# Unread products of the identity on TensorE, ahead of the first round and behind two packs of each of the first eight blocks

## The chip, the cores and the metric

The kernel runs on one core of one Trainium2 chip. The metric is device time in microseconds (us) of one execution, with all loads from and stores to device memory in it. The core has five engines with a queue each: PE (TensorE, matmuls; its weight loads are shown apart as PEld), DVE (VectorE), ACT (ScalarE), POOL (GpSimd) and SP (SyncE, which here only issues transfers). An engine takes the instructions of its queue in order and waits for others by semaphores. PE reads from SBUF and writes to PSUM only.

## The reference

Two parts follow each other. The first is a gated linear recurrence with a 40 x 40 state for each of 4 x 8 (batch, head) pairs over 768 steps; the second is a feed-forward block whose gate mixes along the sequence.

```python
for t in range(S):                                   # S = 768, D = 40
    m_new = np.maximum(f_gate[:, :, t] + m, i_gate[:, :, t])
    f_stab, i_stab = np.exp(f_gate[:, :, t] + m - m_new), np.exp(i_gate[:, :, t] - m_new)
    C = f_stab * C + i_stab * einsum('bhd,bhe->bhde', vt, kt)
    n = f_stab * n + i_stab * kt
    y[:, :, t] = sigmoid(o_gate[:, :, t]) * (C @ qt) / max(abs(n @ qt), 1)
x = y as (4, 768, 320)
h = relu(x @ w_in); u, v = halves of h               # 320 -> 2 x 512
v_n = (v - mean(v)) / sqrt(var(v) + 1e-6)
v_s = einsum('ts,bsd->btd', w_spatial, v_n) + b_spatial
out = (u * v_s) @ w_out                              # 512 -> 320
```

All tensors are float32.

## The kernel before

The recurrence is worked in blocks of 128 steps: 4 batches of 6 blocks, numbered n = 0 to 23, each of two sub-blocks of 64 steps and 8 heads. A block n passes through these packs of small matmuls on PE, and through DVE, ACT and POOL between them:

- `pe_ex(n)` (L364): one matmul of 128 x 512 whose result is the exponent of the weights of the block; ACT makes W from it (L401), POOL scales the keys by W (`ktw`, L406).
- `pe_s(n)` (L370): 16 products of keys and queries into SX; DVE multiplies them by W into KS (`keys`, L415).
- `pe_dc(n)` (L379): 16 products of scaled keys and values into DX, which are the changes of the states; DVE adds them to the decayed states ST (`step`, L431 and L433), which POOL has decayed (L423).
- `pe_intra(n)` (L387): 16 products of KS and values into DX.
- `pe_inter(n)` (L396): 16 products of queries and states into SX.
- `rows(n)` on DVE (L441 reads SX, L445 reads DX), `norm(n)` (L451 to L459), `gated(n)` on POOL (L465, L467), then `turn(n)` (L478): three transposes on PE into px, read by ACT (L484, xH) and DVE (L490, xL).

SX and DX are two PSUM tiles of two banks each, with 512 columns a bank; they have one copy. In SX the products of `pe_s` take columns 0 to 255 of both banks and those of `pe_inter` columns 256 to 419; columns 420 to 511 are used by nothing.

The second part has `a_v` (L528, matmuls of 128 x 512 into pv), a normalisation over DVE, ACT and POOL (L535 to L559), `b_pu` (L570) and `b_pb` (L579 to L581, 128 x 384), and `c_out` (L603 to L605). Its weights are loaded as 64-bit numbers and split into a high and a low half on ACT, DVE and POOL (`conv`, L261 to L283) and `split` (L296 to L298) while the first blocks run. The first `a_v` comes at 67.7 us, the first `b_pb` at 94.4 us.

Ahead of block 0 stand the gates: scans on DVE, then `gates_decay1(z)` for the two halves z of the sequence, which puts three transposes (L175) and one product (L177) on PE, and transfers through device memory that lay the gates out for `pe_ex`.

The order is written out by hand: every function is a generator that yields between instructions, all of them stand in a list `stages`, and a table of numbers, ORDER, says whose next step is issued. Each engine's queue holds its instructions in that order. Waits are found from the tiles: an instruction waits for the earlier ones of other engines that wrote what it reads or read what it writes.

Of the kernel before, what the change touches and what calls it, by code (L numbers as in the profile page):

```python
# [37 lines left out]
def mlstm_moe(ctx: ExitStack, tc: tile.TileContext, a):  # L38
    nc = tc.nc
# [6 lines left out]
    def bank(shape, name):  # L46
        return ps.tile(shape, F32, name=name, tag="pm", bufs=4)


    ident = const.tile([128, 128], F32, name="ident")  # L50
# [114 lines left out]
    def gates_decay1(z):  # L165

        ez = eg[:, z * hs:z * hs + hs]
        dg = wk.tile([128, NB, 16], F32, name="dg", tag="dg", bufs=1)[0:BH]
        nc.gpsimd.tensor_tensor(
            out=dg, in0=ez.rearrange("p (c t) -> p c t", t=L)[:, :, L - 1:L].broadcast_to([BH, NB, 16]),  # L170
            in1=pick[:, 0:16].unsqueeze(1).broadcast_to([BH, NB, 16]), op=ALU.mult)
        yield
        pe = bank([128, 512], "pe")
        for i in range(NB // 2):
            nc.tensor.transpose(pe[:, i * BH:(i + 1) * BH], ez[:, i * 128:(i + 1) * 128], ident[0:BH, 0:BH])  # L175
        pd = pe[:, 128:128 + NB * 16]
        nc.tensor.matmul(pd, pick[:, 16:144], dg.rearrange("p c x -> p (c x)"), start=True, stop=True)  # L177
        dec_[z] = pe, pd

    dec_ = {}  # L180
# [138 lines left out]
    SX = ps.tile([128, 2, 512], F32, name="SX", tag="SX", bufs=1)  # L319
# [4 lines left out]
    intra_ = DX[:, :, 256:256 + HH * E]  # L324
    PAIRS = ((0, 0), (1, 0), (0, 1), (1, 1))

    def rh_v(t):
        return t[:, 0:VW].rearrange("p (h d) -> p h d", h=H)

    def rh_k(t):  # L330
        return t[:, VW:VW + KW].rearrange("p (h d) -> p h d", h=H)
# [4 lines left out]
    def half(p):  # L336
        return slice(64 * p, 64 * p + 64)

    def feat(p):
        return slice(64 * p, 64 * p + D)  # L340
# [32 lines left out]
    def pe_dc(n):  # L373
        rh = RH[n % NRH]
        for j in range(HH):
            for hf, e in PAIRS:
                if n % NB < NB - 1 or e == 0:
                    h, r = hf * HH + j, half(e ^ hf)
                    nc.tensor.matmul(  # L379
                        dc_[feat(hf), e, j * E:(j + 1) * E], rh_k(rh)[r, h], rh_v(rh)[r, h], start=True, stop=True)  # L380

    def pe_intra(n):
        rh, ks = RH[n % NRH], KS[n % NKS]
        for j in range(HH):
            for hf, e in PAIRS:
                h, r = hf * HH + j, half(e ^ hf)
                nc.tensor.matmul(intra_[half(e), hf, j * E:(j + 1) * E], ks[r, h], rh_v(rh)[r, h], start=True, stop=True)  # L387

    def state(n, e):
        return ZS if n % NB == 0 and e == 0 else ST[(2 * n + e) % NST]  # L390
# [101 lines left out]
    def pe_pack(n):  # L492

        if n + 2 < N:
            pe_ex(n + 2)
        if n + 1 < N:
            pe_dc(n + 1)
        if n >= 0:
            pe_intra(n)
        if n + 2 < N:  # L500
            pe_s(n + 2)
        if n >= 0:
            pe_inter(n)
# [132 lines left out]
    def pack(n):  # L636
# [5 lines left out]
        if n + 1 < N:  # L642
            do(pe_dc, n + 1)
            do(step, n + 1, 0)
            do(decay, n + 1, 1)
        if n >= 0:
            do(pe_intra, n)
# [42 lines left out]
    for z in range(2):  # L690
        do(gates_max, z, V)
        do(gates_sum, z)
        do(gates_parts, z, V)
        do(store_g, z, SP)
        do(gates_low, z, V)
        do(load_a_near, z, 0, AQ)
        do(load_a_near, z, 1, PQ)
        if z == 0:
            do(load_g, 0, SP)
            do(load_g, 1, SP)  # L700
            do(load_rh, 1)
            do(load_qk, 2)
        do(gates_exp, z)
        do(gates_decay1, z)
        do(gates_decay2, z)
# [12 lines left out]
    do(weights, 1)  # L718
    do(load_g, 3, SP)
    do(pe_dc, 0)  # L720
    do(pe_s, 1)
    do(step, 0, 0)
# [71 lines left out]
    n, prev = 7, (0, 0, 0)  # L794
# [131 lines left out]
```

## Time and profile before

| | us |
|---|---|
| runs | 377.08, 378.86, 427.2 |
| median of the runs | 378.86 |
| profiled execution, its own time | 378.9 |
| its span, first to last instruction | 377.1 |
| PE busy in the span | 330.6 (88%) |
| PE weight loads busy | 298.9 |
| DVE busy | 220.1 |
| ACT busy | 144.8 |
| POOL busy | 111.7 |
| mean granted TensorE clock, as recorded | 0.982 |

The span is the time in which instructions ran; 1.8 us of the execution's own time lie around it. Busy times are sums over the span, and since the kernel has stages with different limits, they are to be read stage by stage. A matmul's busy time holds its way through the array, so matmuls overlap, and the distance between the starts of neighbours tells what one costs in a row. The granted clock is made from records of its changes; a stretch ahead of the first record shows 1.00 whatever the clock was, so durations of like instructions have to be read beside it.

### The profile page before, as it was taken

What the parts mean: (1) busy time and instruction counts of PE and PEld (TensorE: products, weight loads), DVE (VectorE), ACT (ScalarE), POOL (GpSimd) and SP (SyncE); (2) the same over time, 40 slices, a digit from 0 to 9 for tenths busy, and PEclk for the clock granted to TensorE, in tenths of its full rate; (3) what the DMA queues carried; (4) which work ended last, traced back from release to release, by engine and by line L of the source; (5) the groups of instructions that cost most, each with busy time, mean ns of one, the idle gap of its engine ahead of it and who ended that gap; (6) DMA issues with size and microseconds to landing.
All of it is one profiled execution on the core that took longest, in us unless ns stands there. A gap on an engine that the chain in (4) does not pass through costs nothing.

```text
span 377.1 us, 10595 instructions
## 1 busy us (share of the span) xinstructions
PE 330.6 (88%) x4426; PEld 298.9 (79%) x4426; DVE 220.1 (58%) x552; ACT 144.8 (38%) x335; POOL 111.7 (30%) x178
## 2 busy tenths in 40 slices
PE   0215685989699999999999999999999999999996
PEld 0104574756678899989899999889899998999996
DVE  6556869569779877345767454447675234614231
ACT  6256214267624332367332322663321216701211
POOL 5156645256535244111423232123331101200000
PEclk9999999989869999999999999999999999999999
DMA  7856244554251324300233414002100100100101
GB/s 200 253 155 224 82 127 138 161 171 128 67 170 55 127 86 145 105 2 18 78 94 123 142 56 141 1 20 73 56 2 2 54 1 0 54 0 0 51 5 52
DMA packets 16047, 32.24 MB, mean 85 GB/s; under 512 B 4028, under 2 KB 8920, under 8 KB 16000
## 3 DMA queue, kind: packets, MB, share of 16 engines
q1 hardware_dynamic: 15456, 31.30, 27.3%
q8 instruction: 35, 0.57, 0.6%
q0 software_dynamic: 416, 0.15, 0.2%
q10 hardware_dynamic: 128, 0.12, 0.1%
q14 instruction: 12, 0.10, 0.1%
HBM read 27.19 MB, written 4.33 MB: 84 GB/s over the span
## 4 chain that ended last, share of the span: by engine, by line
PE 80%; DVE 7%; DMA 5%; POOL 3%; issue 2%; SPq 1%; ACT 1%; POOLq 0%; DVEq 0%; ACTq 0%
PE pv L528 12%; PE pu L570 12%; PE pb L579 10%; PE pb L581 9%; PE pb L580 9%; PE DX L387 4%; PE SX L396 4%; PE pc L603 4%; PE pc L605 4%; PE pc L604 4%; PE SX L370 3%; PE px L478 3%; DMA w<-in_w_in 2%; PE DX L379 2%; DMA QK<-in_qk 2%
## 5 line engine op out<-in xcount | busy, mean ns | idle before, releaser
L579 PE MATMUL pb<-wsH,vH 128*128 128x384 f32 x192 | 69.0, 359 | 0.7 <-DVE g L587 0.7
L580 PE MATMUL pb<-wsL,vH 128*128 128x384 f32 x192 | 65.2, 339 | 0.0
L581 PE MATMUL pb<-wsH,vL 128*128 128x384 f32 x192 | 65.0, 339 | 0.0
L591 ACT CAST big<-g 128x384 fp32r<-128x384 f32 x32 | 16.4, 513 | 95.3 <-DVE g L589 93.2
L587 DVE TENSOR_TENSOR g<-pb,bsp 128x384 f32<-128x384 f32 x32 | 17.8, 556 | 43.0 <-PE pb L581 42.7
L579 PEld LDWEIGHTS pb<-wsH,vH 128*128 128x128 f32 x192 | 36.3, 189 | 2.6 <-DVE g L587 1.0
L580 PEld LDWEIGHTS pb<-wsL,vH 128*128 128x128 f32 x192 | 36.5, 190 | 0.2
L581 PEld LDWEIGHTS pb<-wsH,vL 128*128 128x128 f32 x192 | 36.4, 190 | 0.0
L545 POOL TENSOR_TENSOR st<-st,half_neg 128x1 f32<-128x1 f32 x24 | 14.7, 619 | 67.5 <-DVE st L543 64.5
L570 PE MATMUL pu<-xH,wiH 128*128 128x384 f32 x96 | 33.1, 345 | 0.4 <-DVE xL L490 0.4
L423 POOL TENSOR_TENSOR ST<-ST,DEC 104x164 f32<-104x164 f32 x40 | 21.9, 548 | 37.5 <-DVE ST L433 24.7
L528 PE MATMUL pv<-wiH,xH 128*128 128x512 f32 x72 | 30.0, 428 | 0.0
L603 PE MATMUL pc<-woH,big 128*128 128x320 f32 x96 | 29.8, 311 | 0.0
L605 PE MATMUL pc<-woH,big 128*128 128x320 f32 x96 | 29.6, 308 | 0.0
L604 PE MATMUL pc<-woL,big 128*128 128x320 f32 x96 | 29.6, 308 | 0.0
L387 PEld LDWEIGHTS DX<-RH,KS 64*64 64x64 f32 x768 | 15.6, 154 | 13.8 <-DVE ST L433 7.6
L387 PE MATMUL DX<-RH,KS 64*64 64x41 f32 x768 | 18.6, 248 | 8.8 <-DVE ST L433 6.9
L401 ACT ACTIVATE W<-ex 128x512 f32<-128x512 f32 x24 | 14.3, 595 | 31.2 <-PE ex L364 19.0
L406 POOL TENSOR_TENSOR RH<-RH,W 128x320 f32<-128x320 f32 x24 | 17.7, 738 | 28.4 <-ACT W L401 27.7
L370 PE MATMUL SX<-QK 40*64 40x64 f32 x768 | 20.9, 258 | 5.1 <-DVE KS L415 4.7
L484 ACT ACTIVATE xH<-px 128x384 fp32r<-128x384 f32 x24 | 11.8, 490 | 34.4 <-PE px L478 34.3
L415 DVE TENSOR_TENSOR KS<-SX,W 128x512 f32<-128x512 f32 x24 | 16.5, 686 | 14.5 <-PE DX L387 9.5
(120 smaller groups left out, 766.3 us busy)
## 6 DMA issues: line engine op xcount, KB each, us to landing
RH<-in_vk SPq DMA_DIRECT2D x24, 484.0 KB
QK<-in_qk SPq DMA_DIRECT2D x48, 160.0 KB
out<-ot SPq DMA_DIRECT2D x24, 160.0 KB
big<-in_w_sp SPq DMA_DIRECT2D x6, 384.0 KB
w64b<-in_w_out SPq DMA_DIRECT2D x4, 320.0 KB
w<-in_w_in SPq DMA_DIRECT2D x4, 256.0 KB
w64b<-in_w_in SPq DMA_DIRECT2D x4, 256.0 KB
w<-in_w_rem SPq DMA_DIRECT2D x2, 256.0 KB
```

What stands on the lines that cost most here:

```text
L370: nc.tensor.matmul(s_[half(e ^ hf), hf, j * L:(j + 1) * L], QK[feat(hf), e, 0, j], QK[feat(hf), e, 1, j], start=True, stop=True)
L387: nc.tensor.matmul(intra_[half(e), hf, j * E:(j + 1) * E], ks[r, h], rh_v(rh)[r, h], start=True, stop=True)
L423: nc.gpsimd.tensor_tensor(out=ST[(2 * n + e + 1) % NST][0:HI], in0=state(n, e)[0:HI], in1=DEC[0:HI, 2 * k + e, b * HH:(b + 1) * HH].unsque ...
L528: nc.tensor.matmul(pm, l, r, start=i == 0, stop=i == len(terms) - 1)
L570: nc.tensor.matmul(pu, w, x, start=i == 0, stop=i == len(terms) - 1)
L579: nc.tensor.matmul(pb, vH[:, cd], wsH[hf][:, s], start=s == 0, stop=False)
L580: nc.tensor.matmul(pb, vH[:, cd], wsL[hf][:, s], start=False, stop=False)
L581: nc.tensor.matmul(pb, vL[:, cd], wsH[hf][:, s], start=False, stop=s == NB - 1)
L587: nc.vector.tensor_tensor(out=g, in0=pb_[(b, hf, d)], in1=bsp[:, hf * 384:hf * 384 + 384], op=ALU.add)
L603: nc.tensor.matmul(pc, gH[:, c], woH[:, d], start=d == 0, stop=False)
L604: nc.tensor.matmul(pc, gH[:, c], woL[:, d], start=False, stop=False)
L605: nc.tensor.matmul(pc, gL[:, c], woH[:, d], start=False, stop=d == 3)
```

## The change

A function `busy(m)` puts m matmuls of the identity with 92 of its own columns into the unused columns of SX's first bank. Nothing reads the result. It is called with 26 at the end of `gates_decay1(1)`, and with 4 at the end of `pe_dc(n)` and of `pe_intra(n)` for n below 8: 26 + 16 x 4 = 90 products, which are 180 matmuls on PE, since each product of float32 operands is two matmuls with a weight load each (L177 shows it). No `yield` is added, so ORDER fits as it is, and PE's queue is otherwise the same.

```diff
@@ gates_decay1
         nc.tensor.matmul(pd, pick[:, 16:144], dg.rearrange("p c x -> p (c x)"), start=True, stop=True)
+        if z == 1:
+            busy(26)
         dec_[z] = pe, pd
@@ ahead of rh_v
+    def busy(m):
+
+        for _ in range(m):
+            nc.tensor.matmul(SX[:, 0, 420:512], ident, ident[:, 0:92], start=True, stop=True)
+
@@ pe_dc, at its end
+        if n < 8:
+            busy(4)
@@ pe_intra, at its end
+        if n < 8:
+            busy(4)
```

Lines of the changed kernel are numbered 2 to 11 higher than those of the kernel before (L370 is L377, L379 is L386, L387 is L396, L396 is L407, L364 is L371, L415 is L426, L441 is L452); `busy` is L332.

PE's queue at the start. In the kernel before, the last product of the gates is followed by the exponents of blocks 0 and 1 (ex), the keys by queries of block 1, the states' changes of block 0 (DX from RH) and the keys by queries of block 2:

```order
L177 MATMUL pe<-dg,pick 128x96
L364 MATMUL ex<-GM_76,AT_73 128x512
L364 MATMUL ex<-GM_77,AT_73 128x512
L370 MATMUL SX<-QK_107 64x64 x16
L379 MATMUL DX<-RH_102 40x41 x16
L370 MATMUL SX<-QK_108 64x64 x16
```

In the changed kernel:

```order
L177 MATMUL pe<-dg,pick 128x96
L332 MATMUL SX<-ident 128x92 x26
L371 MATMUL ex<-GM_76,AT_73 128x512
L371 MATMUL ex<-GM_77,AT_73 128x512
L377 MATMUL SX<-QK_107 64x64 x16
L386 MATMUL DX<-RH_102 40x41 x16
L332 MATMUL SX<-ident 128x92 x4
L377 MATMUL SX<-QK_108 64x64 x16
```

The 26 products wait for nothing new and stand ahead of both exponents; four more stand between the states' changes of block 0 and the next pack.

PE's queue around block 1, with the waits of each instruction. Before, the states' changes of block 2 (RH_104) are followed by intra of block 1 and by inter of block 2, whose first matmul waits for DVE:

```order
L379 MATMUL DX<-RH_104 40x41 [waits DVE_49,Pool_49]
L379 MATMUL DX<-RH_104 40x41 x15
L387 MATMUL DX<-RH_103,KS_101 64x41 [waits DVE_49]
L387 MATMUL DX<-RH_103,KS_101 64x41 x15
L396 MATMUL SX<-ST_115,QK_108 64x41 [waits DVE_49]
```

In the changed kernel:

```order
L386 MATMUL DX<-RH_104 40x41 [waits DVE_49,Pool_49]
L386 MATMUL DX<-RH_104 40x41 x15
L332 MATMUL SX<-ident 128x92 x4
L396 MATMUL DX<-RH_103,KS_101 64x41 [waits DVE_49]
L396 MATMUL DX<-RH_103,KS_101 64x41 x15
L332 MATMUL SX<-ident 128x92 [waits DVE_49]
L332 MATMUL SX<-ident 128x92 x3
L407 MATMUL SX<-ST_115,QK_108 64x41 [waits DVE_49]
```

Here the products behind intra wait for DVE themselves, since their columns lie between the first and the last column that DVE's last reading of SX spans; the same holds behind intra of blocks 3 and 7.

DVE's queue at the keys of block 1 (KS_101). Before, the multiplication waits for ACT's W alone:

```order
L431 COPY ST_112<-DX 104x164 [waits PE_49]
L280 TENSOR_TENSOR bits<-bits,wiH 64x256 [waits Activation_49]
L415 TENSOR_TENSOR KS_101<-SX,W 128x512 [waits Activation_49]
L433 TENSOR_TENSOR ST_113<-DX,ST_113 104x164 [waits Pool_49]
L298 TENSOR_TENSOR wsL_95<-big,wsH_93 128x384 [waits DMAHW0_49,DVE_49,Activation_49]
```

In the changed kernel:

```order
L442 COPY ST_112<-DX 104x164 [waits PE_49]
L282 TENSOR_TENSOR bits<-bits,wiH 64x256 [waits Activation_49]
L426 TENSOR_TENSOR KS_101<-SX,W 128x512 [waits PE_49,Activation_49]
L444 TENSOR_TENSOR ST_113<-DX,ST_113 104x164 [waits Pool_49]
L300 TENSOR_TENSOR wsL_95<-big,wsH_93 128x384 [waits DMAHW0_49,DVE_49,Activation_49]
```

It now waits for the four products behind the states' changes of block 0 as well. Two later multiplications into KS and two readings of SX by L441 have got such a wait on PE too; their order on DVE is unchanged.

## The prediction

> **What bounds the kernel now.** I read the page's busy shares by slice first, then PE's busy time in stretches of time, then single matmuls, to see at which clock they ran. The page shows PE and the recorded clock in 40 slices of 9.4 us each:
>
> ```profile
> PE   0215685989699999999999999999999999999996
> ...
> PEclk9999999989869999999999999999999999999999
> ```
>
> From about 113 us on PE is full to the end. What the first 113 us lose or gain is therefore added to the end nearly one for one. The stages, each engine's busy time with the number of instructions, then the clock and the transfers:
>
> ```profile
> 20.70:28.27 7.57, 0.00 (x1) 0.03 (x1) 4.72 (x13) 3.81 (x12) 4.30 (x7) 1.00 0.65 179
> 28.27:44.64 16.37, 10.09 (x293) 8.13 (x293) 13.06 (x31) 8.06 (x19) 10.58 (x14) 1.00 0.49 158
> 44.64:62.24 17.60, 12.29 (x301) 10.11 (x301) 13.30 (x33) 5.75 (x13) 8.50 (x15) 1.00 0.48 139
> 62.24:76.48 14.24, 13.35 (x164) 10.09 (x164) 8.23 (x22) 3.63 (x9) 4.08 (x6) 1.00 0.50 152
> ...
> 83.31:100.38 17.07, 13.62 (x195) 10.29 (x195) 16.17 (x41) 11.62 (x28) 10.70 (x16) 1.00 0.32 84
> ```
>
> Before 28 us PE waits for the gates. From 28 to 62 us PE (22.4 of 34.0 us) and DVE (26.4) take turns, from 62 to 76 us PE is the bound, and from 83 to 100 us DVE is (16.2 of 17.1). Now the clock. Three matmuls of one shape, start and duration:
>
> ```profile
> 73.42 0.63 PE L528 MATMUL pv<-wiH,xH 128*128 128x512 f32 x1
> ...
> 81.56 0.63 PE L528 MATMUL pv<-wiH,xL 128*128 128x512 f32 x1
> ...
> 83.83 0.39 PE L528 MATMUL pv<-wiH,xH 128*128 128x512 f32 x1
> ```
>
> The second ran at a recorded 0.50 and the third at 1.00 (rows below). The first is as slow as the second, though the column says 1.00: nothing is recorded ahead of the first change. So PE ran at half speed until about 76 us, and the change's 90 unread products can be meant for nothing but this clock, or cost time. The records change on a grid of 3.41 us, so I cut PE's busy time along it:
>
> ```profile
> 69.66:73.07 3.41, 3.41 (x39) 1.00 0.18 59
> 73.07:76.48 3.41, 3.41 (x9) 1.00 0.72 203
> 76.48:79.90 3.42, 1.59 (x97) 1.00 0.49 148
> 79.90:83.31 3.41, 3.41 (x52) 0.50 0.72 243
> ...
> 100.38:103.79 3.41, 3.41 (x97) 0.50 0.31 126
> 103.79:107.21 3.42, 3.42 (x69) 0.50 0.28 78
> 107.21:110.62 3.41, 3.41 (x42) 0.50 0.84 241
> ```
>
> Two things are to be seen. A full window need not raise the clock: those from 69.66, 100.38 and 103.79 were full, held many small matmuls, and left it low; those from 73.07, 79.90 and 107.21, with mostly wide ones, were followed by a high clock. And a window with 1.59 of 3.42 us busy was followed by a low one, though its longest gap was the 1.8 us of the waits below.
>
> **What a product costs.** The nearest rows are the gates' product, float32 with the same 128 weight columns and 96 instead of 92 columns moving, and the transposes:
>
> ```profile
> 19.96 0.52 PE L177 MATMUL pe<-dg,pick 32*128 32x96 f32 x1
> ...
> 19.96 0.74 PE L177 MATMUL pe<-dg,pick 32*128 32x96 f32 x2
> ...
> 54.87 0.90 PE L478 MATMUL px<-ident,x 128*128 128x128 f32 x3
> 55.42 0.78 PE L364 MATMUL ex<-GM,AT 84*128 84x512 f32 x1
> ```
>
> L177's first matmul ends at 20.48 and the second at 20.70: 0.22 us each at the low clock, rounded to 0.43 a product. Bounds: two transposes' distance, 2 x (55.42 - 54.87)/3 = 0.37 us, and the pair alone from start to end, 0.74, which counts the way through the array that followers share. I take 0.43, since shape and type are L177's; at the high clock half, 0.21, as pv's duration falls. Four are 1.7 us low, 0.9 high.
>
> **The 26 at the start.** They need only the identity, which L175 has used, and begin behind L177's second matmul at about 20.3 us. At the low clock they take 26 x 0.43 = 11.2 us, to 31.5. Their cover is PE's wait for a transfer, up to 28.27, and behind it the next cover is ACT:
>
> ```profile
> 28.27 1.19 PE L364 MATMUL ex<-GM,AT 84*128 84x512 f32 x2 [7.57 <-DMA GM<-scr_g]
> ...
> 30.13 0.59 ACT L401 ACTIVATE W<-ex 128x512 f32<-128x512 f32 x1
> ```
>
> ex would start 3.2 us late. ACT takes it at 30.13, and could have done so from about 28.9 (0.6 us for the first of the two), so 1.2 us of the 3.2 are hidden and W is 2.0 late; with it the keys on DVE and everything behind them. If the clock rises after some 5 us of the 26, they end near 28.5 and cost nothing. I take 2.0.
>
> **The 16 packs.** Behind the states' changes or intra the four products run in PE's next wait, if there is one. The waits of PE from 28.27 to 62.24 us, then from 62.2 to 101 us (total, times, longest):
>
> ```profile
> PE SX L370 <- DVE KS L415: 4.7, 3, 2.0
> PE DX L387 <- DVE ST L433: 2.9, 3, 1.4
> PE SX L396 <- DVE xs L441: 1.5, 1, 1.5
> PE DX L379 <- POOL RH L406: 1.2, 1, 1.2
> PE SX L396 <- DVE KS L415: 0.9, 1, 0.9
> PE px L478 <- POOL x L467: 0.4, 1, 0.4
> ...
> PE DX L387 <- DVE ST L433: 4.0, 2, 3.1
> PE DX L387 <- DVE ST L431: 1.8, 1, 1.8
> ```
>
> Blocks 0 to 3: 8 packs of 1.7 us are 13.7. Cover: 4.7 less the 2.0 ahead of the first pack and less about 1.0 that stands behind ex (the keys that end it are made from that ex, so the wait moves along); 2.9; 1.5; 0.4. That is 6.5. The 0.9 is none, because there the products wait for the same DVE instruction first. On the path: 13.7 - 6.5 = 7.2 us. New waits come with it: the keys and L441 on DVE wait for products they don't read, and behind them stand the states' changes on DVE and then POOL.
>
> Blocks 4 to 7: the packs behind changes 5, 6 and 7 and intra 4, 5, 6 and 7 (the eighth, behind changes 4, fell into the part above). Five at the low clock, two (changes 6, intra 6) at the high: 5 x 1.7 + 2 x 0.9 = 10.3. Cover: 1.2 and 0.9 (the first of the 4.0), and 0.9 where DVE is the bound behind intra 6. The 1.8 is no cover, since the pack of changes 6 stands ahead of block 7's keys by queries, for which DVE waits first. On the path 7.3 us.
>
> Back comes some clock: a window like that from 76.48 is filled by 0.9 us more and may keep the clock (half of 3.4 us), and the gap of 3.1 us ahead of 100 may fall across two windows (half of 10.2). I count 2.5 of these 6.8.
>
> Sum: 2.0 + 7.2 + 7.3 - 2.5 = 14.0 us on the profiled execution's own 378.9 (span 377.1 and 1.8 around it), which lies 0.04 above the median of the runs: 393 us. No transfer is added, none moves in SP's or POOL's queue; loads that wait for a buffer go later with the blocks, and none is late for PE in these rows.
>
> This rests on the clock not staying high, and here I weigh a rule. Between 28.3 and 34 us PE would hold, at the high clock, ex 0.6, two packs of 16 at 0.5 and four products, about 2.5 us in 5.7: less than the 47% of the window after which the clock fell. So even if the 26 raise it, I expect it to fall there. The Trainium skill, "TensorE: Matmul & The Clock Gate", Part 1: The HAM clock gate, says that the low clock is the default, that some 3.4 us of sustained matmuls release it, and that an idle window brings it back. By that rule the 26 would raise it and gaps of 2 us would not end it, which gives the first rival's time. The rows agree on the default and the window's length; on the release, three full windows disagree, and on the fall the window from 76.48 does, which was not idle.
>
> **The rivals.** First, faster: the clock rises during the 26 and stays. Its place is the gap from 28.3 to 34 us, and it decides whether the clock survives that. For it: the 26 leave PE no gap, as in the windows that raised it; against it: the three full windows, and the fall. Price: the start costs nothing; PE's and DVE's turns from 28 to 62 us gain about 3.3 (PE's share of a round halves by some 2.3 us a block, the products give 1.7 back, DVE keeps the rest); 62.24 to 76.48 gains half of 13.35, 6.7; 79.90 to 83.31 gains 1.7; seven packs at 0.9 cost 6.0; half of a chance at the 5.1 from 100.38 on is 2.5. Together -8.2: 371 us.
>
> Second, no change: the products cost less than L177 says, because the weights are the same each time, and fall into waits. For it: the waits of 28 to 62 us sum to 11.5. With 0.2 a product, at either clock, 16 packs are 13 us, 10 of them hidden; with 1 or 2 us of clock won, 378 to 383 us.
>
> Third, the change does nothing to PE's order but lengthen it, with the clock raised for a few us at the start: the forecast without its 2.0, 391. I count it with the forecast.
>
> **How the numbers follow.** Forecast with the third: 0.57; its own range is 384 (all the clock comes back, 0.37 a product) to 402 (none comes back and DVE's new waits take half the cover). Faster rival: 0.30, from 366 to 377. Second: 0.13. A measurement of this kernel tells 2% from no change, so the marks are 371.3 and 386.5. Faster by over 2%: 0.20 from the first rival and 0.02 from the second. Slower: 0.54 of the 0.57. The rest, 0.24, within. The range of 370 to 401 leaves out a third of the first rival (0.11) and 0.05 at the top.
>
> **What would show it.** Right: pv at 0.63 us in its first eight, DX and SX packs of 16 around 1.1 us from 30 to 60 us; ex of block 0 starting near 31.5; `busy` lines near 0.4 us apart; the first b_pb later than 94.4 us by about 14. Wrong: packs of 0.7 us and pv of 0.39 from the first one on, ex at 28.3, and PE's waits for DVE longer than before; then the clock stayed high and the first rival holds. If packs are slow and the end comes within 4 us, the waits hid more than 6.5.

## The result and the profile after

| us | before | after |
|---|---|---|
| median of 4 runs each | 377.97 | 400.1 |
| lowest to highest of the undisturbed runs | 376.03 to 378.86 | 396.41 to 400.26 |
| ratio, with its 95% interval | | 1.057 (1.046 to 1.068) |
| span of the profiled execution | 377.1 | 394.6 |
| PE busy in it | 330.6 | 360.5 |

The changed kernel is slower by 5.7%. The second row and the ratio leave out one run of each kernel, 427.2 before and 402.62 after, which lie over 1.5% above the fastest of their kernel. The profiled execution is the fastest of its four: its span grew by 17.5 us, while the medians lie 22 apart. The page's lines that answer to those quoted ahead, busy PE and the recorded clock in 40 slices, here of 9.9 us each:

```profile
PE 360.5 (91%) x4606; PEld 329.6 (84%) x4606; DVE 218.8 (55%) x552; ACT 145.2 (37%) x335; POOL 111.3 (28%) x178
...
PE   0298798998969999999999999999999999999996
...
PEclk9999999998986999999999999999999999999999
```

PE is nearly full from the third slice on, where before it had waits between 28 and 62 us. It is full of unread products and not of more useful work, as PE's timeline shows (start, duration; in brackets the idle time ahead and who ended it):

```profile
20.48 11.40 PE L332 MATMUL SX<-ident 128*128 128x92 f32 x52
31.59 1.20 PE L371 MATMUL ex<-GM,AT 84*128 84x512 f32 x2
33.78 1.13 PE L377 MATMUL SX<-QK 40*64 40x64 f32 x32 [0.99 <-DVE KS L426]
34.68 0.77 PE L386 MATMUL DX<-RH 64*40 64x41 f32 x32
35.38 2.01 PE L332 MATMUL SX<-ident 128*128 128x92 f32 x8
38.25 1.14 PE L377 MATMUL SX<-QK 40*64 40x64 f32 x32 [0.85 <-DVE KS L426]
```

The 26 products take 11 us, ex follows at 31.6, and a pack of 16 small products (x32, two matmuls each) still takes 1.1 us: the clock is low, as it was. The same place in the chain of work that ended last (start, duration):

```profile
35.45 1.96 PE SX L332 x8
37.41 0.03 issue
37.46 0.04 issue
37.51 0.70 DVE KS L426
...
40.75 1.96 PE SX L332 x8
42.70 0.02 issue
42.73 0.50 DVE xs L452
```

A pack of four unread products stands on the chain (in what follows, a pack is four unread products unless its line is named), and DVE's keys (L426) and its reading of SX (L452), which read none of its columns, start within 0.1 us of its end. Summed up, what DVE and then what PE waited for from 31.7 to 73.0 us, that is between ex of block 0 and intra of block 3 (total, times, longest):

```profile
DVE KS L426 <- PE SX L332: 6.7, 3, 3.0
DVE xs L452 <- PE SX L332: 5.5, 3, 3.8
```

```profile
PE SX L377 <- DVE KS L426: 2.9, 3, 1.0
PE SX L407 <- DVE xs L452: 1.5, 1, 1.5
PE DX L396 <- DVE ST L444: 1.0, 1, 1.0
PE SX L407 <- DVE KS L426: 0.9, 1, 0.9
```

The waits of DVE that a pack ended sum to 12.2 us; a part of them would be there without the pack, since DVE also waited for work that stands ahead of it on PE. PE still waits 6.3 us for DVE. The same part as one stretch each, first before and then after (length, PE busy, weight loads, DVE, ACT, POOL, clock, transfers):

```profile
28.27:58.27 30.00, 19.96 (x557) 16.48 (x557) 22.39 (x56) 12.11 (x27) 16.30 (x24) 1.00 0.49 153
```

```profile
31.59:72.79 41.20, 34.95 (x622) 30.62 (x621) 20.05 (x48) 11.00 (x24) 15.68 (x24) 1.00 0.26 79
```

The part grew by 11.2 us: PE's busy time by 15.0, for eight packs, and its idle time fell only from 10.0 to 6.3. Of these 3.8, 1.0 is the wait ahead of the first pack (2.03 before, 0.99 after), which the start took up. Where the two executions stand at the same work, by the starts of PE's instructions in the two timelines:

| start of | before | after | later by |
|---|---|---|---|
| ex of block 0 | 28.27 | 31.59 | 3.3 |
| states' changes of block 0 | 32.40 | 34.68 | 2.3 |
| intra of block 3 | 58.27 | 72.79 | 14.5 |
| first pv | 67.67 | 82.83 | 15.2 |
| 17th pv | 80.56 | 94.36 | 13.8 |
| first b_pb | 94.43 | 108.14 | 13.7 |
| 19th b_pb | 112.81 | 128.80 | 16.0 |
| last b_pb | 368.94 | 386.46 | 17.5 |

From 72.79 us to the first b_pb nothing more was lost, though seven packs stand there. The rows of pv (duration least, median, most) tell why:

```profile
L539 PE MATMUL pv<-wiH,xH x8: 394/398/622, 82.8 to 95.3; 128*128 128x512 f32 x8
```

Before, nearly all of those ahead of 76.5 us took 0.63 us each. After, the same work comes 15 us later, while the recorded clock rose at nearly the same time (77.6 us against 76.5), so it runs at 0.39. That is in part the luck of this execution. Here the clock rose 5.2 us ahead of the first pv; in the profiled executions of before and of the kernels e1, e3, e4, e7 and e8 below it rose 3 to 9 us behind it. The two later stretches of low clock came back as long as they were, 3.4 and 10.2 us; the windows ahead of them and their own first windows:

```profile
87.83:91.24 3.41, 2.29 (x81) 2.02 (x84) 1.46 (x6) 3.29 (x9) 1.98 (x4) 1.00 0.90 281
91.24:94.66 3.42, 3.42 (x44) 3.34 (x43) 1.23 (x6) 0.50 (x3) 1.44 (x3) 0.50 0.69 244
111.73:115.14 3.41, 0.74 (x33) 0.69 (x34) 3.35 (x8) 1.39 (x4) 1.31 (x3) 1.00 0.42 121
115.14:118.55 3.41, 3.41 (x72) 3.25 (x72) 0.40 (x1) 2.27 (x6) 1.42 (x2) 0.50 0.08 29
```

### The profile page after: what moved, and what is told of

Same layout as the page of the kernel before. It is cut to its first block, busy times and chain, and to the rows that moved or that the text cites. A ratio compares the mean times of both kernels' runs of the same rounds, so it can differ in the third digit from the quotient of the medians.

```text
span 394.6 us, 10957 instructions
## 1 busy us (share of the span) xinstructions
PE 360.5 (91%) x4606; PEld 329.6 (84%) x4606; DVE 218.8 (55%) x552; ACT 145.2 (37%) x335; POOL 111.3 (28%) x178
## 4 chain that ended last, share of the span: by engine, by line
PE 85%; DMA 5%; DVE 4%; ACT 2%; POOL 1%; issue 1%; SPq 1%; ACTq 0%; DVEq 0%
PE pu L581 11%; PE pv L539 10%; PE pb L590 10%; PE SX L332 9%; PE pb L592 8%; PE pb L591 8%; PE DX L396 4%; PE SX L377 4%; PE SX L407 4%; PE pc L614 4%; PE pc L616 3%; DMA QK<-in_qk 3%; PE pc L615 3%; PE px L489 3%; PE DX L386 2%; DMA RH<-in_vk 2%
## 5 line engine op out<-in xcount | busy, mean ns | idle before, releaser
L332 PE MATMUL SX<-ident 128*128 128x92 f32 x180 | 39.1, 397 | 0.0
L332 PEld LDWEIGHTS SX<-ident 128*128 128x128 f32 x180 | 35.5, 298 | 1.3 <-issue 0.2
L426 DVE TENSOR_TENSOR KS<-SX,W 128x512 f32<-128x512 f32 x24 | 16.5, 688 | 25.1 <-PE SX L332 9.2
L539 PE MATMUL pv<-wiH,xH 128*128 128x512 f32 x72 | 28.0, 401 | 0.0
L396 PEld LDWEIGHTS DX<-RH,KS 64*64 64x64 f32 x768 | 15.6, 151 | 12.0 <-DVE ST L444 5.1
```

The lines of the kernel that those rows point to most:

```text
L332: nc.tensor.matmul(SX[:, 0, 420:512], ident, ident[:, 0:92], start=True, stop=True)
L539: nc.tensor.matmul(pm, l, r, start=i == 0, stop=i == len(terms) - 1)
```

## Experiments

The products are read by nothing, so every kernel here computes all of the reference. The median of before is 376.45 us (e1 to e4), 376.27 (e5 to e8) and 377.34 (e9, e10) on the chips used.

**e1, the start alone.** 26 products ahead of the first round and no packs, against the changed kernel:

```diff
         if z == 1:
             busy(26)
...
-        if n < 8:
-            busy(4)
```

> Only the 26 products at the start, no packs. Theory (the 26 leave the clock low and overrun PE's wait): they take 11.1 us (52 matmuls, 0.213 us apart), the first exponent starts at 31.5 to 31.7 us instead of 28.3, the first W 2 to 2.5 us later, the whole 2 to 3 us longer than before (380 to 381); pv's first eight matmuls keep 0.63 us. Rival (they raise the clock, and the packs' gaps lost it again): matmuls of 0.39 to 0.5 us among the 26 or behind them, and a time at or below that of before.

Measured 379.48 us, ratio 1.009 (1.005 to 1.012). Its products, by duration, first and last start:

```profile
L332 PE MATMUL SX<-ident x52: 421/421/522, 20.6 to 31.5; 128*128 128x92 f32 x52
```

51 distances in 10.9 us are 0.21 us for a matmul and 0.43 for a product. No matmul was faster than the first ones: 11 us of a full PE left the clock low. Both the states' changes of block 0 and the first pv come 2.4 us late (70.04 against 67.67 for the latter). Behind that the clock rose 2.6 us sooner than before (at 73.9 us) and was low for less time (from 80.7 to 84.1 and from 101.2 to 104.6 us, 6.8 in place of 13.6), and the profiled execution ended 1.0 earlier than the one before, while the medians are 3.0 slower.

**e2, the packs alone.** The call with 26 is taken out, the 16 packs stay.

```diff
-        if z == 1:
-            busy(26)
```

> Only the 16 packs of four, not the 26. Theory (PE's queue plus the waits of DVE's readers of SX for the packs ahead of them): the changed kernel's 17.5 us of span less the start's 2.3, so about 15 us over before. Rival (PE's queue alone, with PE's waits of before as cover, as the prediction had it): 7.2 + 7.3 - 2.5 = 12 us over before.

Measured 396.81 us, ratio 1.050 (1.044 to 1.057): some 20 us for the packs, more than the 15 and the 12 of the two forecasts. With the 0.9% of e1 this gives 5.9%, and the whole change has 5.7% (4.6 to 6.8), so the two parts add up within the intervals, and the packs hold some 85% of the loss.

**e3 and e4, waits for unread columns.** Eight packs, behind intra only, in SX as the change has them (e3), or in unused columns of DX (e4), which the keys on DVE do not read.

```diff
-            nc.tensor.matmul(SX[:, 0, 420:512], ident, ident[:, 0:92], start=True, stop=True)
+            nc.tensor.matmul(DX[:, 0, 420:512], ident, ident[:, 0:92], start=True, stop=True)
```

> Only the eight packs behind intra, written to SX as in the change. Theory (DVE's multiplications into KS for blocks 3, 4 and 6 and their followers wait for the pack in SX though they read other columns): about 9 us over before, and these multiplications start within 0.15 us of the end of a pack. Rival (PE's queue alone): 7 us, the same as the next run.

> The same eight packs, written to unused columns of DX instead of SX, which the multiplications into KS don't read. Theory (waits for a tile that isn't needed): the multiplications into KS run beside the pack instead of behind it, some 0.7 us saved at each of three to four places, so 2 to 3 us less than the run with SX, 6 to 7 over before. Rival (PE's queue alone): within 1 us of the run with SX.

Measured 389.54 us (e3), ratio 1.036 (1.031 to 1.040), and 388.83 (e4), ratio 1.034 (1.030 to 1.038): 13.1 and 12.4 us over before, more than either forecast of either run. DVE's waits for the packs from 36 to 76 us, in e3 and then in e4:

```profile
DVE KS L422 <- PE SX L330: 8.7, 3, 3.0
```

```profile
DVE xs L452 <- PE DX L330: 3.5, 3, 1.2
```

With DX no wait of the keys is ended by a pack. L452 is in e4 DVE's reading of DX (L445 before); its waits are ended by packs instead, for 3.5 us, and those of L440, which reads DX for the states, for another 1.2. So e4 has moved these waits and made them shorter, and no run has products in a tile that nobody reads. At inter of block 3, with three packs ahead of it, e3 is 5.5 us later than before and e4 4.1, so at least 1.4 of the 5.5 are the price of DVE's waits. At the end the two are 0.7 us apart, in intervals that overlap, as the rival of e4 had it: in these profiles e4's second low stretch was the longer one (10.2 us against 6.8), and e4 lost its lead there and at pv.

What PE waited for in e3 from 28 to 66 us, whose lines answer to those of before quoted in the prediction:

```profile
PE SX L375 <- DVE KS L422: 5.7, 3, 3.0
PE DX L392 <- DVE ST L440: 2.9, 3, 1.4
PE SX L403 <- DVE xs L448: 1.5, 1, 1.5
PE SX L403 <- DVE KS L422: 0.9, 1, 0.9
```

The last three are as long as before. The first has grown from 4.7 only because ex of block 0 started 1.0 us earlier in this execution. So these packs hid in none of PE's waits: the three ahead of intra of block 3 delayed it by 5.5 us, 1.8 each.

**e5 and e6, could the start have raised the clock?** The 26 products move 92 columns for each load of 128 weight columns. e5 moves 256 columns for a load (13 products, no packs), e6 keeps the 92 and loads 64 weight columns (36 products, no packs).

In e5:

```diff
-            nc.tensor.matmul(SX[:, 0, 420:512], ident, ident[:, 0:92], start=True, stop=True)
+            nc.tensor.matmul(SX[:, 0, 256:512].rearrange("p (a c) -> p a c", a=2), ident, ident.unsqueeze(1).broadcast_to([128, 2, 128]), start=True, stop=True)
```

In e6:

```diff
-            nc.tensor.matmul(SX[:, 0, 420:512], ident, ident[:, 0:92], start=True, stop=True)
+            nc.tensor.matmul(SX[0:64, 0, 420:512], ident[:, 0:64], ident[:, 0:92], start=True, stop=True)
```

> Only a start, with 13 products of 256 moving columns instead of 26 of 92 (the identity twice, into SX columns nothing has used yet); 11.1 us at the low clock either way. [...] Time within 1% of before. Rival (float32 products of the identity, or work ahead of the first round, don't release it): spacing stays 0.43 us a matmul to the end at 31.6 us, ex starts at 31.6 to 31.8.

> Only a start, with 36 products of 64 weight columns and 92 moving columns, about 0.15 us a matmul, so that the moving never stops but only half of the array's columns are in use (share of time 1.0, share of array 0.5). Theory (share of the array): the clock stays low through all 36, to about 31.5 us. Rival (share of time in which anything moves): it rises within two windows.

Measured 376.44 us (e5), ratio 1.002 (0.9996 to 1.005), and 376.95 (e6), ratio 1.003 (0.999 to 1.006). The clock rose in both, at 25.5 and 26.7 us, and the timeline of e6 shows the next packs at the high clock, then again at the low:

```profile
21.45 8.46 PE L332 MATMUL SX<-ident 128*64 128x92 f32 x72
29.83 0.73 PE L371 MATMUL ex<-GM,AT 84*128 84x512 f32 x2
32.34 0.69 PE L377 MATMUL SX<-QK 40*64 40x64 f32 x32 [1.77 <-DVE KS L422]
32.86 0.49 PE L386 MATMUL DX<-RH 64*40 64x41 f32 x32
34.97 1.13 PE L377 MATMUL SX<-QK 40*64 40x64 f32 x32 [1.62 <-DVE KS L422]
```

It fell at 32.3 (e5) and 33.6 us (e6), and at the end nothing was gained. The clock records put the fall behind these windows, e5's and e6's:

```profile
28.80:32.20 3.40, 1.28 (x65) 0.85 (x65) 3.11 (x7) 2.98 (x8) 1.95 (x3) 1.00 1.03 332
```

```profile
30.20:33.60 3.40, 1.38 (x66) 0.89 (x64) 2.83 (x7) 3.26 (x8) 2.24 (x3) 0.99 0.85 257
```

e6 decides between two ways of reading the release. It uses half of the array's columns and the clock rose, so the share of the array that is in use does not decide. What remains is the time in which columns move. The matmuls of e5 and the weight loads of e6, both ahead of the rise (durations, first and last start):

```profile
L332 PE MATMUL SX<-ident x8: 634/634/635, 21.5 to 24.5; 128*128 128x256 f32 x8
```

```profile
L332 PEld LDWEIGHTS SX<-ident x34: 181/230/231, 21.4 to 26.4; 128*64 128x64 f32 x34
```

In e5 the matmuls follow each other at 0.43 us (3.0 us in 7 distances), which is 1.67 ns for each of 256 moving columns. In e6 the loads, and with them the matmuls, follow at 0.15 us (5.0 us in 33), which is 1.65 ns for each of 92. Nearly the same price of a column in both says that the moving columns set the pace there. With 128 weight columns e1's matmuls of 92 moving columns follow at 0.21. So in the 26, columns move for some 71% of the time. That the rest goes to the weight load, and that this keeps the clock low, fits these three shapes and is not shown beyond them.

**e7 and e8, products only in two long gaps.** The share that e7's expectation speaks of is the share of the array that is in use over a clock window. Before, the low stretch from 100.4 us followed the gap of 3.1 us ahead of it. e7 puts 12 products behind the states' changes of block 8 only, e8 six more behind the keys by queries of block 7.

The call in `pe_dc`, with the tile as a second argument, and the one that e8 has in `pe_s` as well:

```diff
@@ pe_dc, at its end
+        if n == 8:
+            busy(12, SX)
@@ pe_s, at its end
+        if n == 7:
+            busy(6, DX)
```

> The kernel before with only 12 products behind the states' changes of block 8, where PE waited 3.1 us for DVE at 97 us. Theory (the clock falls behind a window of a share below about 0.35 and stays above 0.4): 12 x 0.213 = 2.6 us run inside the wait, the window keeps 0.5 or more, the clock stays high from 83 us on, and the 10 us at half clock of the kernel before at 100 us are gone: 3 to 5 us faster. Rival (the products delay DVE's readers of SX and PE as the packs did, or the clock falls all the same): within 1 us of before or slower.

> As the run before, with six more products, into DX, behind block 7's keys by queries, where PE waited 1.8 us at 77.6 us. Theory: 1.3 us of them are hidden, the window keeps about 0.45 instead of 0.29, and the fall at 80 us (3.4 us at half clock) is gone too: 1.5 us better than the run before. Rival: the states' copy on DVE waits for them and intra of block 5 is late by as much: no better or worse.

Measured 373.03 us (e7) and 373.53 (e8), both with a ratio of 0.994 (0.991 to 0.997). The clock in 40 slices, of e7 and then of e8:

```profile
PEclk9999999989999999999999999999999999999999
```

```profile
PEclk9999999999999999999999999999999999999999
```

In e7 the stretch at 100 us is gone and the profiled execution ends 3.4 us earlier, though it is the slowest of e7's twelve. All twelve recorded a mean clock of 0.995 or 1.000, the runs of before 0.981 to 0.990. So the gap that was filled is the one behind which the clock fell, as e7's theory had it. In e8 the other stretch is gone as well and its profiled execution ends 2.3 us before e7's, but the medians of the two are the same, as e8's rival had it. Its profile had its lead ahead of its first product: the states' changes of block 6 start 2.5 us sooner than in e7, since the clock rose at 71.4 us and not at 77.0. So no gain is shown for the second gap. These two are the fastest kernels of the study, faster than before and after. The start of these changes in e7 and in e8:

```profile
77.25 0.52 PE L384 MATMUL DX<-RH 64*40 64x41 f32 x32
```

```profile
74.70 0.52 PE L386 MATMUL DX<-RH 64*40 64x41 f32 x32
```

**e9 and e10, could packs hold the clock?** The start of e6 and, at the change's 16 places, four (e9) or eight (e10) products of 64 weight columns, behind intra in DX; e10 has eight behind the second exponent too.

The calls of e10; e9 has 4 for each 8 and not the one in `pe_ex`:

```diff
@@ pe_ex, at its end
+        if n == 1:
+            busy(8, DX)
@@ pe_dc, at its end
+        if n < 8:
+            busy(8, SX)
@@ pe_intra, at its end
+        if n < 8:
+            busy(8, DX)
```

> The kernel before with the start of 36 products of 64 weight columns, which raised the clock at 26.8 us, and with 4 such products behind each pack of states' changes (in SX) and of intra (in DX) for blocks 0 to 7. A product is 0.31 us at the low clock and 0.15 at the high one, so four are 1.2 or 0.6. Theory (the clock falls in the gap behind the start, since a window must hold columns moving for more than about a third of it, and four narrow products add 0.6 of 3.4 us): it falls near 33.6 us as before, the packs then cost 1.2 us each of which some 0.8 stay on the path up to block 4, and the time is 383 to 389 us. Rival (the packs hold the clock): ex, SX and DX packs of 16 at 0.5 to 0.6 us up to 62 us, pv at 0.39 from the first one on, 368 to 373 us.

> The same with 8 products of 64 weight columns instead of 4 at each of the 16 places, and 8 behind the second exponent, where PE waits for DVE. Theory (share of a window in which columns move decides): 8 such products at the high clock move columns for 1.2 us, so a window of 3.4 us with one pack and 16 small matmuls lies at about 0.5 and the clock holds from 26 us on; pv at 0.39 from the first one on. The packs then cost 1.2 us each, as much as the blocks' own small matmuls gain up to 62 us, and 62 to 76 us gains about 6.7 less 5 for its packs: 372 to 379 us. Rival (only wide or long matmuls hold it, or the gaps of 2 us end it): it falls near 33 us, packs of 2.5 us at the low clock, 395 to 408 us.

Measured 381.92 us (e9), ratio 1.012 (1.006 to 1.019), and 380.56 (e10), ratio 1.010 (1.005 to 1.016). In e9 the clock fell at 31.8 us, rose again at 52.3 and fell at 65.9. So neither forecast holds: it fell in the gap behind the start, ahead of the first pack at 33.9 us, but with the packs it rose behind a window in which PE was full (3.42 of 3.42 us from 48.9). In e10 it held from 26.6 to 64.1 us, as the theory had it, and the time came out just above the theory's 372 to 379. Windows of e10, the emptiest that held and the one behind which it fell, and the row of pv:

```profile
40.25:43.67 3.42, 2.19 (x53) 1.64 (x52) 2.65 (x8) 1.09 (x2) 1.48 (x3) 1.00 0.04 11
...
60.73:64.15 3.42, 1.88 (x30) 1.40 (x29) 3.13 (x9) 1.70 (x4) 1.35 (x2) 1.00 0.59 171
```

```profile
L541 PE MATMUL pv<-wiH,xH x6: 392/395/504, 70.8 to 75.0; 128*128 128x512 f32 x6
```

The states' changes of block 4 start 0.8 us later than before, with eight packs of 1.4 us each ahead of them. So the high clock and the waits together took up all but 0.8 of some 11 us of products, and behind it the kernel is 1.0% slower. Holding the clock through these blocks is possible; at this price it does not pay.

## Why the prediction came out as it did

**The direction and the low clock: right, and shown.** Forecast 393 us with a range to 401; measured 400.1, near the top of it. The clock stayed low to 77.6 us, with packs of small matmuls at 1.1 us and the first long gain at pv.

**A product's price: right.** 0.43 us was taken from L177's two ends; e1 shows 0.43.

**The start, +2.0: right, +2.3.** ACT's cover hid 1.0 of the 3.3, not 1.2. e1 alone gives 2.4 at the same step and at the first pv.

**Packs of blocks 0 to 3, +7.2: mis-sized; it measured 12.2** (14.5 at intra of block 3, with eight packs ahead of it, less the 2.3). The same stretch, from the states' changes of block 0 to intra of block 3, before and after:

```profile
32.40:58.27 25.87, 17.87 (x533) 15.10 (x527) 19.18 (x46) 8.79 (x20) 13.90 (x22) 1.00 0.40 120
```

```profile
34.68:72.79 38.11, 32.84 (x597) 29.24 (x590) 18.69 (x45) 8.80 (x20) 14.37 (x23) 1.00 0.25 74
```

PE's busy time grew by 15.0, where the term has 13.7. The term put four products at 1.7 us, by the distance between matmuls; on the chain a pack takes 1.96 or 1.94. PE's idle time fell by 2.7, where the term has a cover of 6.5. These two, 1.3 and 3.8, are the 5 us that the term lacks. The cover was taken from a list of PE's waits as if each stayed where it was. But the waits are for DVE instructions that are themselves behind an earlier pack, either because they wait for it by the tile or because PE issues later what they need, so a wait moves along with the delay. e3 shows this plainly, with PE's waits as long as before; e4 shows that DVE's waits by the tile cost at least 1.4 of 5.5 there. The prediction named these waits of DVE, put nothing for them into the 7.2, and had them take half the cover only at the slow end of its range.

**Packs of blocks 4 to 7 less the clock given back, +4.8: too high for its place, -0.8 to the first b_pb and +3.0 to the end.** Its count is one short: up to 62.24 us there stand nine packs (behind the changes of blocks 0 to 4 and intra of 0 to 3), of which the sum prices eight, and seven come behind, so one of the 16, 1.7 us by its own price, is in no term. The clock that came back was not in the windows that the prediction named. The stretches of 3.4 and 10.2 us stayed. The gain came from the lateness itself: the work that ran at the low clock from 62 to 76.5 us, whose gain the prediction had put at 6.7 us under its first rival, now ran almost all behind the rise. So the sum of 14.0 came as near as it did to the 17.5 of the profile in part by luck: a gain that was not forecast set off some of the cover that was not there and of the pack that was not counted.

Of the last 1.5 (16.0 at the 19th b_pb, 17.5 at the last) the profile shows 0.9 in two places, at 205 and 291 us, where PE stood still in the midst of a pack of intra without a cause that it names. Why the other three executions are 3.5 to 6.2 us slower than the profiled one stays open. Their mean recorded clock is the same (0.982 to 0.983), but it counts the stretch ahead of the first record as 1.00, so a later first rise would not show in it.

**The clock gate: right in the outcome.** The prediction said that the clock, if raised, would fall between 28 and 34 us; e5 and e6, which have no packs, raised it and it fell at 32.3 and 33.6. The first rival, a clock that rises in the 26 and stays, failed twice: these 26 do not raise it (e1), and where a start does raise it, it does not stay (e5, e6). Its price was also too good, as far as e10 tells, whose products are narrower and more: with the clock held to 64 us the time was 380.6 and not 371. A start that raises the clock was not run with the packs of the change. On the release the Trainium skill, "TensorE: Matmul & The Clock Gate", Part 1: The HAM clock gate, says that about 3.4 us of sustained matmuls release the low clock. e5 and e6 agree, with a rise within two windows; the change itself disagrees, with 11 us of matmuls without a gap and no rise. On the fall, the same section of the Trainium skill speaks of an idle window; here the clock fell behind windows in which PE was busy for 1.28 to 2.29 of 3.4 us, so no idle window was needed.

**The second rival, cheaper products in waits:** ruled out by the price of 0.43 (e1), and by the waits, which took 2.7 us of the eight packs up to intra of block 3, where it needs 10 for all 16. The third, a clock raised for a few us at the start, failed with e1.

## What to carry to other kernels

A list of waits is not a budget for filler: a wait whose releaser stands behind the filler moves with it, so count as cover only waits whose releaser does not depend on the engine that is filled, and let the filler write to a tile whose readers come late (e4 was 1.4 us ahead of e3 by that; a tile that nobody reads was not tried). If a clock is to be raised or kept by extra matmuls, look for the single gap behind which it falls and fill only that (e7: 12 products, 0.6% faster). Here products at every round cost as much as the clock returned (e10) or far more (the change). A few us of delay or gain ahead of a clock window can come back or vanish behind it, so compare starts of the same work through the whole run and not the ends of two profiles.

## What was not expected of the hardware

A PE that is busy without a gap need not raise its clock: 52 matmuls of 128 x 92 with 128 weight columns (11 us) left it low, while 72 with 64 weight columns and 26 with 256 moving columns raised it after 4 to 6 us. In these runs that goes with the time in which columns move; only these three shapes were tried by themselves. Nor does the work alone say when the clock rises: before, e7 and e8 have the same instructions on PE up to 75 us, and it rose at 76.5, 77.0 and 71.4 us. And the clock falls with PE far from idle. Of the windows quoted here, at the high clock, those with 0.74, 1.28, 1.38, 1.59, 1.88 and 2.29 us busy of 3.4 were followed by a low clock, and one with 2.19 was not, so the busy time alone does not draw the line exactly.
